# Bias groups in pairs behind the values, first scores before the ninth group, and finishing transposes right behind those of the probabilities

## The chip, the cores and the metric

The kernel runs on one core of a Trainium2 chip. The core has five engines that run at the same time and wait for each other by semaphores: TensorE (PE: matmuls and transposes; PEld is its loading of weights), VectorE (DVE), ScalarE (ACT), GpSimd (POOL) and SyncE (SP), which here issues nearly all transfers between HBM and the on-chip memory SBUF. Matmuls write to PSUM, eight banks per partition; VectorE and ScalarE read them there. The metric is the device time of one execution in microseconds (us), the median of several runs.

## The reference

Attention with a bias that depends on the positions, then two feed-forward layers. B = 2, H = 8, S = 576, D = 64, a hidden size of 32 for the bias.

```python
scores = scale * q @ k^T                                   # per batch and head, 576 x 576
x = log1p(|i - j|) / log1p(max(i, 1))                      # 576 x 576
bias = relu(x * w1 + b1) @ w2                              # 32 hidden, one bias per head
attn = softmax(scores + bias) ; out = attn @ v
x = out as (1152 tokens, 512)
x = (silu(xn @ w_gate) * (xn @ w_val)) @ w_out             # xn: RMS-normed x, 512 -> 1536 -> 512
return (s * relu(x @ w_in)**2 + b) @ w_out2                # 512 -> 2048 -> 512
```

## The kernel before

**Attention.** The work is cut into 36 units: nine tiles of 128 queries, four pairs of heads each (unit u is pair u % 4 of tile u // 4). A loop over steps s = -2 to 36, written out by hand, sets the order on every engine, since each engine runs its instructions in program order. Step s does the scores of unit s + 1 (`scores_mm`, L236, into two PSUM tiles of the ring `psA`), its softmax (`soft` on VectorE, L249, adds the bias and gives the row's extreme; `expo` on ScalarE, L257), the transposes of the probabilities of unit s (`turn_mm`, nine transposes, L266 and L268, in three PSUM tiles; `turn_out`, L274, copies the first and the third to SBUF on ScalarE, the second on VectorE) and the values of unit s - 1 (`values_mm`, L294).

**Finishing a tile of queries.** When the four units of tile p are through, `finish_a` (ScalarE copies `po`, at the start of a step with s % 4 = 1), `finish_t` (four transposes, L307, same step), `finish_b`, `finish_s` and `finish_n` (VectorE: division, norm) and `finish_c` (four transposes back, L339, in a step with s % 4 = 0, from step 8 on) bring the tile into the layout of the feed-forward part.

**PSUM.** The bias groups from 8 on, the transposes of the probabilities and those of the finish all take their tiles from one ring of three buffers, `psB`, in program order: a tile waits until the one three places earlier has been read.

**The bias.** The 576 rows come in 36 groups of 16. `hidden(g)` writes four hidden rows of group g ("quads", L168): on VectorE, but the third on ScalarE for g < 8 and the fourth on GpSimd for g >= 8. `bias_mm(g)` multiplies them with w2 (L181, 8 instructions; the wider g is from the middle, the more columns, 304 to 576), `bias_out(g)` scales them on ScalarE (L197) and stores them: groups 0 to 7 right into the SBUF bias tile (L205), the others to HBM (`rows`, L201), from where a later step's `bias_in` loads them in the shape of the scores (L215). A load waits for the store of its rows. One bias tile serves eight units; its eight groups must be there before the first of them.

**What is in the way of what.** `plan[s]` says which groups' matmuls come in step s: groups 0 to 8 in step -2, then one a step up to group 35 in step 25, at the start of the step, ahead of the scores. SP issues in program order the keys (`load_k`, 288 KB a unit, needed for units 0 to 7), the values (`load_v`, 320 KB), rows (295.5 KB) and bias loads (288 KB a group); an entry that waits holds all behind it.

**Feed-forward.** From about 189 us TensorE does the two feed-forward layers with split weights (L531 to L533); the change doesn't touch them.

Of the kernel before, what the change touches and what calls it, by code (L numbers as in the profile page):

```python
# [8 lines left out]
F32 = mybir.dt.float32  # L9
# [8 lines left out]
P = 128  # L18
# [19 lines left out]
SCALE = 8.0  # L38
AHD = 9
LEAD = 3  # L40
# [9 lines left out]
def tile_kernel(ctx: ExitStack, tc: tile.TileContext, q, k, v, ltab, lg, cst, cst2, rms_g, wg, wv, wo, win, wo2, s_p, b_p, out):  # L50
# [105 lines left out]
    def hidden(g):  # L156
        hms[g] = []
        d = reach(g)
        for tq in range(4):
# [4 lines left out]
            if tq == ACT_QUAD and g in ACT_EARLY:  # L164
                nc.scalar.activation(hq, src, AF.Relu, bias=nthr[:, n:n + 1], scale=w1_sb)
                continue
            eng = nc.gpsimd if tq == POOL_QUAD and g >= 8 else nc.vector
            eng.tensor_scalar(hq, src, w1_sb, thr[:, n:n + 1], op0=ALU.mult, op1=ALU.max)  # L168
# [230 lines left out]
    for g in range(AHD, NG):  # L399
        plan[g - 10 if g >= 16 else g - AHD - 1].append(g)  # L400

    def hide(g):
        if g < NG:
            hidden(g)

    AHEAD = {6: (load_k, 1), 8: (load_v, 0)}
    TAIL = [(22, w_fetch, 0), (22, w_fetch, 1), (27, w_clamp, 0), (28, w_clamp, 1), (31, w_split, 0), (31, w_fetch, 2),
# [3 lines left out]
    for g in range(LEAD):  # L411
        hide(g)
    for s in range(-2, NU + 1):
        r = s % 4
# [8 lines left out]
        landed = list(rows)  # L423
        for g in plan[s]:
            pb = bias_mm(g)
            if g == 0:
                pcb = psB.tile([P, 512], F32, name="b")
                nc.tensor.matmul(pcb[:, 0:1], c2_sb[:, :P], c2_sb[:, P:], start=True, stop=True)
                nc.scalar.activation(cb[:, 0:1], pcb[:, 0:1], AF.Copy, scale=SCALE)
                nc.scalar.activation(cb[:, 1:2], pcb[:, 0:1], AF.Copy, scale=m_sb)  # L430
            bias_out(g, pb)
            if g in AHEAD:
                AHEAD[g][0](AHEAD[g][1])
            if s == -2:
                hide(g + LEAD)
        for g in landed:
            bias_in(g)
        if s >= 6 and r == 2:
            finish_b(s // 4 - 1)
# [20 lines left out]
        if s >= 7 and r == 3:  # L460
            finish_n(s // 4 - 1)
        if plan[s] and s >= -1:
            hide(plan[s][-1] + LEAD)
        if s == 0:
            nc.sync.dma_start(out=g_bc, in_=rms_g.partition_broadcast(P))
            nc.sync.dma_start(out=s_sb, in_=s_p)
            nc.sync.dma_start(out=b_sb, in_=b_p)
        if 0 <= s - 1 < NU:
            values_mm(s - 1)
        if s >= 5 and r == 1:  # L470
# [3 lines left out]
        if s >= 8 and r == 0:  # L474
            finish_c(s // 4 - 2)
        if s == 26:
            gen.close()
            wpools["ab"] = ring(ctx, "wab", 2)
            wpools["sp"] = ring(ctx, "wsp", 4)
# [261 lines left out]
```

## Time and profile before

| | |
|---|---|
| median of 3 runs | 620.36 us (620.31 to 620.48) |
| profiled execution | 620.82 us, of which the span of instructions is 619.0 us |
| mean granted TensorE clock | 0.994 |
| busy, share of the span | TensorE 98%, VectorE 65%, ScalarE 50%, GpSimd 33% |
| HBM | 53.47 MB read, 10.83 MB written |

Times below are us from the span's start. "Idle before" in square brackets is the time the engine stood still ahead of a row, with what ended it. The granted clock is the share of TensorE's full clock of 2.4 GHz; 0.5 is its lower level, 1.2 GHz. Ends of matmuls are modelled, so how long a piece of TensorE's work takes is read from the start of one row to the start of the next.

### The profile page before, as it was taken

What the parts mean: (1) busy time and instruction counts of PE and PEld (TensorE: products, weight loads), DVE (VectorE), ACT (ScalarE), POOL (GpSimd) and SP (SyncE); (2) the same over time, 40 slices, a digit from 0 to 9 for tenths busy, and PEclk for the clock granted to TensorE, in tenths of its full rate; (3) what the DMA queues carried; (4) which work ended last, traced back from release to release, by engine and by line L of the source; (5) the groups of instructions that cost most, each with busy time, mean ns of one, the idle gap of its engine ahead of it and who ended that gap; (6) DMA issues with size and microseconds to landing.
All of it is one profiled execution on the core that took longest, in us unless ns stands there. A gap on an engine that the chain in (4) does not pass through costs nothing.

```text
span 619.0 us, 11231 instructions
## 1 busy us (share of the span) xinstructions
PE 607.4 (98%) x4368; PEld 545.4 (88%) x4368; DVE 403.5 (65%) x748; ACT 309.3 (50%) x644; POOL 204.8 (33%) x180
## 2 busy tenths in 40 slices
PE   8699999999999999999999999999999999999997
PEld 5266666666779999999999999999999999999997
DVE  7587898976787555555545555547777635778841
ACT  7387777777775344434443223225555325555310
POOL 0933355530013333333333233223233423232430
PEclk9799999999999999999999999999999999999999
DMA  5699554558021222222231322222212331221431
GB/s 150 183 304 289 155 153 134 155 179 224 11 69 55 84 88 89 98 68 74 98 102 69 103 76 96 69 69 80 90 69 78 128 103 40 96 69 68 141 100 51
DMA packets 25877, 67.39 MB, mean 109 GB/s; under 512 B 3136, under 2 KB 4704, under 8 KB 25824
## 3 DMA queue, kind: packets, MB, share of 16 engines
q1 hardware_dynamic: 25632, 66.37, 34.3%
q8 instruction: 34, 0.56, 0.4%
q10 hardware_dynamic: 192, 0.31, 0.2%
q14 instruction: 19, 0.16, 0.1%
HBM read 53.47 MB, written 10.83 MB: 104 GB/s over the span
## 4 chain that ended last, share of the span: by engine, by line
PE 75%; DVE 13%; ACT 5%; issue 4%; DMA 1%; POOL 1%; SPq 0%; DVEq 0%; POOLq 0%
PE c L531 9%; PE c L532 9%; PE c L533 9%; PE b L533 7%; PE b L531 7%; PE b L532 7%; PE po L294 6%; PE a L236 6%; PE b L266 5%; DVE f L600 4%; DVE hv L596 4%; PE b L181 3%; ACT f L599 3%; PE po L531 2%; PE po L533 2%
## 5 line engine op out<-in xcount | busy, mean ns | idle before, releaser
L391 POOL TENSOR_TENSOR wlo<-ww,whi 128x512 fp32r<-128x512 f32 x68 | 96.5, 1420 | 101.1 <-ACT whi L390 101.1
L369 POOL TENSOR_SCALAR wa<-wa 128x512 f32<-128x512 f32 x68 | 44.2, 650 | 182.8 <-ACT wa L368 180.3
L168 POOL TENSOR_SCALAR hq<-tab,c_sb,thr 128x448 f32<-128x448 f32 (+17 forms) x28 | 57.7, 2065 | 40.2 <-PE b L181 26.2
L249 DVE CUSTOM_DVE_ANT_0 sn<-a,bias 128x576 f32<-128x576 f32 x72 | 51.7, 753 | 28.5 <-PE a L236 22.8
L375 DVE TENSOR_SCALAR wa<-wa 128x512 int32<-128x512 int32 x68 | 37.6, 553 | 40.1 <-POOL wa L369 40.1
L257 ACT ACTIVATE pr<-sn,nm 128x576 f32<-128x576 f32 x72 | 56.1, 780 | 6.2 <-DVE nm L249 6.1
L368 ACT ACTIVATE wa<-wraw 128x512 f32<-128x512 f32 x68 | 45.3, 666 | 27.4 <-DMA wraw<-in_wo 24.9
L533 PE MATMUL c<-f,wlo 128*128 128x384 f32 (+1 forms) x168 | 55.7, 332 | 0.0
L532 PE MATMUL c<-f,whi 128*128 128x384 f32 (+1 forms) x168 | 55.7, 332 | 0.0
L531 PE MATMUL c<-f,whi 128*128 128x384 f32 (+1 forms) x168 | 55.7, 332 | 0.0
L376 DVE SCALAR_TENSOR_TENSOR ww<-wraw,wa 128x512 int32<-128x512 int32 x68 | 52.7, 775 | 3.5 <-issue 0.4
L600 DVE SCALAR_TENSOR_TENSOR f<-hv,b_sb,f 128x384 fp32r<-128x384 f32 x48 | 39.2, 818 | 21.9 <-ACT f L599 21.9
L378 DVE SCALAR_TENSOR_TENSOR ww<-wraw,ww 128x512 int32<-128x512 int32 x68 | 51.9, 763 | 2.3
L599 ACT ACTIVATE f<-hv,b_sb 128x384 fp32r<-128x384 f32 x48 | 29.6, 617 | 45.1 <-DVE hv L596 45.0
L532 PE MATMUL c<-xs,whi 128*128 128x384 f32 x144 | 48.3, 335 | 0.0
L390 ACT CAST whi<-ww 128x512 fp32r<-128x512 f32 x68 | 41.8, 615 | 12.9 <-DVE ww L378 12.9
L531 PE MATMUL c<-xs,whi 128*128 128x384 f32 x144 | 48.2, 335 | 0.0
L533 PE MATMUL c<-xs,wlo 128*128 128x384 f32 x144 | 48.1, 334 | 0.0
L294 PE MATMUL po<-pt,vs 128*64 128x128 f32 (+1 forms) x800 | 47.3, 267 | 0.0
L236 PE MATMUL a<-ks,q 64*128 64x288 f32 (+1 forms) x320 | 46.4, 432 | 0.0
L533 PE MATMUL b<-f,wlo 128*128 128x384 f32 (+1 forms) x132 | 44.8, 339 | 0.4 <-POOL wlo L391 0.4
L532 PE MATMUL b<-f,whi 128*128 128x384 f32 (+1 forms) x132 | 44.6, 338 | 0.0
(121 smaller groups left out, 1481.7 us busy)
## 6 DMA issues: line engine op xcount, KB each, us to landing
wraw<-in_wo SPq DMA_DIRECT2D x28, 512.0 KB, 3.3
bias<-rows SPq DMA_DIRECT2D x32, 288.0 KB, 4.4
rows<-br SPq DMA_DIRECT2D x28, 295.5 KB, 3.2
wraw<-in_win SPq DMA_DIRECT2D x16, 512.0 KB, 3.3
wraw<-in_wg SPq DMA_DIRECT2D x12, 512.0 KB, 3.3
wraw<-in_wv SPq DMA_DIRECT2D x12, 512.0 KB, 3.3
vs<-in_v SPq DMA_DIRECT2D x8, 320.0 KB, 5.3
ks<-in_k SPq DMA_DIRECT2D x8, 288.0 KB, 5.7
```

Source lines behind the costliest of these rows:

```text
L168: eng.tensor_scalar(hq, src, w1_sb, thr[:, n:n + 1], op0=ALU.mult, op1=ALU.max)
L236: nc.tensor.matmul(ps[e][qc, f, :HF], qt[u // 4][ed, hp, qc], ks[b * NP + hp][ed, f * HF:(f + 1) * HF], start=True, stop=True, tile_positi ...
L249: nc.vector.tensor_tensor_reduce(out=sn, in0=ps[:, :, :HF], in1=bias[chunk(u)][:, h, :].rearrange("p (f c) -> p f c", f=2), scale=-1.0 / S ...
L257: nc.scalar.activation(prs[u][:, e * S:(e + 1) * S], sn.rearrange("p f c -> p (f c)"), AF.Exp, bias=nm, scale=-1.0, accum_out=sums[u // 4] ...
L294: nc.tensor.matmul(dst, w, a, start=c == 0, stop=c == NQC - 1, tile_position=(0, e * D))
L376: yield nc.vector.scalar_tensor_tensor(out=w, in0=raw[:, :, 1], scalar=-0x40000000, in1=a, op0=ALU.bitwise_and, op1=ALU.bitwise_or)
L378: yield nc.vector.scalar_tensor_tensor(out=w, in0=raw[:, :, 0], scalar=29, in1=w, op0=ALU.logical_shift_right, op1=ALU.bitwise_or)
L391: nc.gpsimd.tensor_tensor(out=lo, in0=w.bitcast(F32), in1=hi.bitcast(F32), op=ALU.subtract)
L531: nc.tensor.matmul(ps, hi[:, ws], ah, start=first, stop=False)
L532: nc.tensor.matmul(ps, hi[:, ws], al, start=False, stop=False)
L533: nc.tensor.matmul(ps, lo[:, ws], ah, start=False, stop=last)
L600: nc.vector.scalar_tensor_tensor(out=hl[:, cols(j)], in0=g2, scalar=b_sb, in1=hh[:, cols(j)].bitcast(F32), op0=ALU.add, op1=ALU.subtract)
```

## The change

Four things are moved. (1) Step -2 has groups 0 to 7 only; groups 8 and 9 come in step -1, behind the first scores, and GpSimd writes its quarter of the hidden rows only from group 11 on. (2) From group 10 to 31 two groups come together, in every second step (10 and 11 in step 0, 12 and 13 in step 2, ..., 30 and 31 in step 20); groups 32 to 35 keep their steps. (3) The groups of a step stand at its end, behind the values, not ahead of the scores; hidden rows are written for group s + 12 in step s. (4) `finish_t` and `finish_c` stand ahead of the values, right behind the transposes of the probabilities. The keys of unit 1 are loaded behind group 7 instead of 6, the first values behind group 9 instead of 8.

```diff
-AHD = 9
+AHD = 8
+POOL_FROM = 11
...
-            eng = nc.gpsimd if tq == POOL_QUAD and g >= 8 else nc.vector
+            eng = nc.gpsimd if tq == POOL_QUAD and g >= POOL_FROM else nc.vector
...
-        plan[g - 10 if g >= 16 else g - AHD - 1].append(g)
+        plan[g - 10 if g >= 32 else max(g - g % 2 - 10, -1)].append(g)
...
-    AHEAD = {6: (load_k, 1), 8: (load_v, 0)}
+    AHEAD = {7: (load_k, 1), 9: (load_v, 0)}
...
+    def groups(s):
+        for g in plan[s]:
+            pb = bias_mm(g)
...
+            bias_out(g, pb)
+            if s == -2:
+                hide(g + LEAD)
+            if g in AHEAD:
+                AHEAD[g][0](AHEAD[g][1])
...
-        for g in plan[s]:
-            pb = bias_mm(g)
...
         for g in landed:
             bias_in(g)
+        if s == -2:
+            groups(s)
...
-        if plan[s] and s >= -1:
-            hide(plan[s][-1] + LEAD)
+        if s >= -1:
+            hide(s + 12)
...
-        if 0 <= s - 1 < NU:
-            values_mm(s - 1)
         if s >= 5 and r == 1:
             finish_t(s // 4 - 1)
...
         if s >= 8 and r == 0:
             finish_c(s // 4 - 2)
+        if 0 <= s - 1 < NU:
+            values_mm(s - 1)
+        if s >= -1:
+            groups(s)
```

TensorE at the start, before: the last groups of step -2, the first scores (`ks0`), group 10 at the start of step 0 and so on (line, operation, tile written <- tiles read, shape of the result, count).

```order
L181 MATMUL a<-hq,c_sb 32x512 x4
L181 MATMUL a<-hq,c_sb 32x64 x4
L181 MATMUL b<-hq,c_sb 32x448 x4
L181 MATMUL b<-hq,c_sb 32x432 x4
L236 MATMUL a<-ks_127,q 128x288 x4
L181 MATMUL b<-hq,c_sb 32x416 x4
L236 MATMUL a<-ks_309,q 128x288 x4
L266 MATMUL b<-ident,pr 128x128 x8
L268 MATMUL b<-ident,pr 128x128
L181 MATMUL b<-hq,c_sb 32x400 x4
```

The same place of the changed kernel:

```order
L182 MATMUL a<-hq,c_sb 32x512 x4
L182 MATMUL a<-hq,c_sb 32x64 x4
L237 MATMUL a<-ks_127,q 128x288 x4
L182 MATMUL b<-hq,c_sb 32x448 x4
L182 MATMUL b<-hq,c_sb 32x432 x4
L237 MATMUL a<-ks_337,q 128x288 x4
L267 MATMUL b<-ident,pr 128x128 x8
L269 MATMUL b<-ident,pr 128x128
L182 MATMUL b<-hq,c_sb 32x416 x4
L182 MATMUL b<-hq,c_sb 32x400 x4
```

The first scores have moved ahead of groups 8 (448 columns) and 9 (432), and groups 10 and 11 (416 and 400) stand together behind the transposes of unit 0.

TensorE in a step with `finish_t`, before (`pt` and `vs` are probabilities and values, `oT` the tile that is turned; seven more rows of values are left out):

```order
L236 MATMUL a<-ks_593,q 128x288 x4
L266 MATMUL b<-ident,pr 128x128 x8
L268 MATMUL b<-ident,pr 128x128
L294 MATMUL po<-pt_690,vs_591 64x128
...
L294 MATMUL po<-pt_705,vs_591 64x128 x2
L307 MATMUL b<-ident,oT 128x128 x4
L181 MATMUL b<-hq,c_sb 32x320 x4
L236 MATMUL a<-ks_662,q 128x288 x4
```

A later step of the same kind in the changed kernel:

```order
L182 MATMUL b<-hq,c_sb 32x304 x4
L182 MATMUL b<-hq,c_sb 32x320 x4
L237 MATMUL a<-ks_339,q 128x288 x4
L267 MATMUL b<-ident,pr 128x128 x8
L269 MATMUL b<-ident,pr 128x128
L308 MATMUL b<-ident,oT 128x128 x4
L295 MATMUL po<-pt_948,vs_385 64x128
...
L295 MATMUL po<-pt_963,vs_385 64x128 x2
L237 MATMUL a<-ks_339,q 128x288 x4
```

The four transposes have moved from behind the values to the place right behind the nine of the probabilities; two groups of the bias stand together ahead of this step and none behind it.

SP up to the keys of unit 4 (`ks4`), before, from the store of group 8's rows on (buffer numbers kept; `br` is the scaled group, `g_bc` and two small constants are left out):

```order
L201 DMA rows8_347<-br_344 128x591
L134 DMA vs0_349<-in_v 128x640
L130 DMA ks2_359<-in_k 128x576
L201 DMA rows9_369<-br_366 128x591
L215 DMA bias_371<-rows8_347 16x8x576
L126 DMA q_397<-in_q 128x512
L134 DMA vs1_399<-in_v 128x640
L130 DMA ks3_401<-in_k 128x576
L201 DMA rows10_411<-br_408 128x591
L215 DMA bias_371<-rows9_369 16x8x576
...
L134 DMA vs2_458<-in_v 128x640
L130 DMA ks4_460<-in_k 128x576
```

The same in the changed kernel, from the keys of unit 2 on:

```order
L131 DMA ks2_339<-in_k 128x576
L202 DMA rows8_373<-br_370 128x591
...
L135 DMA vs1_389<-in_v 128x640
L131 DMA ks3_391<-in_k 128x576
L216 DMA bias_393<-rows8_373 16x8x576
L216 DMA bias_393<-rows9_383 16x8x576
...
L202 DMA rows10_448<-br_445 128x591
L202 DMA rows11_458<-br_455 128x591
L135 DMA vs2_460<-in_v 128x640
L131 DMA ks4_462<-in_k 128x576
```

The keys of unit 2 have moved ahead of the first rows, and the rows of group 11 now stand ahead of the keys of unit 4; the other transfers between are the same.

## Rows read from the trace of the kernel before

**Rows 1.** The page: TensorE's busy tenths in 40 slices of the span.

```profile
PE   8699999999999999999999999999999999999997
```

**Rows 2.** Stages: busy us (x instructions) by engine, granted clock, DMA share, GB/s.

```profile
18.00:24.00 6.00, 1.56 (x11) 0.34 (x10) 3.72 (x10) 0.83 (x1) 6.00 (x2) 0.81 0.79 192
...
28.00:42.00 14.00, 13.85 (x128) 8.36 (x125) 12.01 (x30) 10.94 (x28) 7.07 (x5) 0.98 0.98 301
...
64.00:130.00 66.00, 65.96 (x662) 43.99 (x662) 59.39 (x141) 52.46 (x125) 30.25 (x17) 1.00 0.50 147
```

**Rows 3.** Timeline of GpSimd, 15 to 22 us: start, us, instruction, [idle before].

```profile
15.21 8.24 POOL L168 TENSOR_SCALAR hq<-tab,c_sb,thr 128x448 f32<-128x448 f32 x1 [13.89 <-DMA bias<-br]
```

**Rows 4.** Timeline of all engines, 0 to 36 us (x: instructions merged).

```profile
16.71 5.02 DVE L168 TENSOR_SCALAR hq<-tab,c_sb,thr 128x448 f32<-128x448 f32 x12
...
19.10 0.54 SPq L205 DMA_DIRECT2D bias<-br  x1
23.50 0.20 PEld L181 LDWEIGHTS b<-hq,c_sb 128*32 128x32 f32 x8 [5.25 <-POOL hq L168]
...
25.30 1.09 ACT L197 ACTIVATE br<-b,cb,c_sb 128x448 f32<-128x448 f32 x2 [6.34 <-PE b L181]
...
28.97 0.76 DVE L249 CUSTOM_DVE_ANT_0 sn<-a,bias 128x576 f32<-128x576 f32 x1 [7.25 <-PE a L236]
...
30.55 0.76 ACT L257 ACTIVATE pr<-sn,nm 128x576 f32<-128x576 f32 x1
```

**Rows 5.** The bias tile, 0 to 40 us: its transfers from issue to landing.

```profile
DMA to landing us min/median/max: 3.2/4.3/6.3
```

**Rows 6.** Timeline of SP, 0 to 75 us: when transfers are issued.

```profile
26.41 0.34 SPq L201 DMA_DIRECT2D rows<-br  x1
...
36.11 0.33 SPq L130 DMA_DIRECT2D ks<-in_k  x1
```

**Rows 7.** DMA issues of 28 to 62 us: count, KB each, median us to landing.

```profile
ks<-in_k SPq DMA_DIRECT2D x5, 288.0 KB, 5.7
```

**Rows 8.** Timeline of TensorE, 36 to 47 us.

```profile
42.40 1.24 PE L236 MATMUL a<-ks,q 64*128 64x288 f32 x8
...
45.95 0.80 PE L181 MATMUL b<-hq,c_sb 128*32 128x352 f32 x8
46.68 0.51 PE L236 MATMUL a<-ks,q 64*128 64x288 f32 x2
```

**Rows 9.** Timeline of TensorE, 86 to 97 us.

```profile
86.47 0.66 PE L339 MATMUL b<-ident,x 128*128 128x128 f32 x4
87.06 0.85 PE L181 MATMUL b<-hq,c_sb 128*32 128x384 f32 x8
87.84 1.24 PE L236 MATMUL a<-ks,q 64*128 64x288 f32 x8
89.01 1.09 PE L266 MATMUL b<-ident,pr 128*128 128x128 f32 x8
...
90.14 1.31 PE L294 MATMUL po<-pt,vs 128*64 128x128 f32 x20
```

**Rows 10.** Timeline of all engines, 82.8 to 86.5 us: the step before.

```profile
84.84 0.58 ACT L274 COPY pt<-b 128x512 f32<-128x512 f32 x1 [0.67 <-PE b L266]
85.02 0.27 PE L268 MATMUL b<-ident,pr 128*128 128x128 f32 x1
...
85.23 1.31 PE L294 MATMUL po<-pt,vs 128*64 128x128 f32 x20
```

**Rows 11.** Timeline of TensorE, 117 to 124.5 us: a group of 496 columns.

```profile
119.69 1.04 PE L181 MATMUL b<-hq,c_sb 128*32 128x496 f32 x8
120.66 1.24 PE L236 MATMUL a<-ks,q 64*128 64x288 f32 x8
```

**Rows 12.** Timeline of TensorE, 58.5 to 66 us.

```profile
64.13 1.62 PE L236 MATMUL a<-ks,q 64*128 64x288 f32 x8
```

**Rows 13.** Timeline of TensorE, 126 to 192 us.

```profile
140.74 0.29 PE L181 MATMUL b<-hq,c_sb 128*32 128x48 f32 x8 [0.56 <-DVE pt L274]
```

More of the change, by code (lines that the diff above doesn't have):

```diff
@@ L412, in tile_kernel @@
         hide(g)
+    def groups(s):
+        for g in plan[s]:
+            pb = bias_mm(g)
+            if g == 0:
+                pcb = psB.tile([P, 512], F32, name="b")
+                nc.tensor.matmul(pcb[:, 0:1], c2_sb[:, :P], c2_sb[:, P:], start=True, stop=True)
+                nc.scalar.activation(cb[:, 0:1], pcb[:, 0:1], AF.Copy, scale=SCALE)
+                nc.scalar.activation(cb[:, 1:2], pcb[:, 0:1], AF.Copy, scale=m_sb)
+            bias_out(g, pb)
[3 more added lines that the diff above has]
+                AHEAD[g][0](AHEAD[g][1])
     for s in range(-2, NU + 1):
@@ L423, in tile_kernel @@
         landed = list(rows)
-        for g in plan[s]:
-            pb = bias_mm(g)
[L426 to L435, printed above, removed]
         for g in landed:
             bias_in(g)
+        if s == -2:
+            groups(s)
         if s >= 6 and r == 2:
```

## The prediction

> **What bounds the kernel now.** I read the slices of the span first [rows 1]: after the first 40 us TensorE is at 0.9 or more in nearly every slice. The stages say the same [rows 2]: from 64 to 130 us TensorE has work in 65.96 of 66 us while VectorE has 59.39 and ScalarE 52.46. So in the attention steps time is gained or lost where TensorE's own row of work gets longer or shorter, or where something makes it stand still. It stands still at the start: from 18 to 24 us it works 1.56 of 6 us at a granted clock of 0.81, and from 28 to 42 us it is the DMA engines that are full (0.98 of the time, 301 GB/s) [rows 2].
>
> The hole at the start is a chain. GpSimd's first hidden row (group 8) starts at 15.21 and takes 8.24 us [rows 3]: VectorE writes its twelve hidden rows in 5.02 us from 16.71 [rows 4], and GpSimd is done only 1.7 us after that run. TensorE's weight load for group 8 waited 5.25 us for it, until 23.50, and the first softmax piece starts at 28.97, 7.25 us after VectorE fell idle [rows 4].
>
> **Part 1, the start.** Now the four hidden rows of groups 8, 9 and 10 are all VectorE's. That is twelve again (three of four groups before), so they end at about 21.7 as before. The first scores come ahead of groups 8 and 9: they start when group 7 is written out, about 19.1 (the last bias piece is issued at 19.10 [rows 4]), and the first softmax piece then waits for that piece: the median landing of these is 4.3 us [rows 5], so 23.4, at most 25.4 (by 6.3). Against 28.97 this is 5.6 us earlier. It costs something: ScalarE now has the write-outs of groups 8 and 9, 1.09 us each for two instructions [rows 4], behind two exponentials and ahead of the first probability copies, so 5.6 - 2.2 = 3.4 us of head start remain. VectorE's run of twelve then meets a GpSimd row (group 11) at its end at most.
>
> **Part 2, who catches up with the head start.** Every unit of scores needs its keys. The keys of unit 4 are issued at 36.11 [rows 6]; with the median landing of 5.7 us [rows 7] they are there at 41.8, and the scores that read them start at 42.40 [rows 8]: 0.6 us of slack while the DMA engines are full. In the new order of SP the transfers from the first bias rows (group 8) to these keys are the same but two: the keys of unit 2 went earlier, into the gap in which the DMA engines were idle, and the rows of group 11 now stand ahead. Both are some 290 KB, so the full stretch is as long. It starts when the rows of group 8 are stored: before at 26.41 [rows 6], now at 23.4 + 2.3 (from the first softmax piece at 28.97 to the end of the second exponential at 31.31 [rows 4]) + 1.1 = 26.8, some tenths later for the issue. So the keys land at about 42.4 and those scores start at 42.5, against 42.40: the 3.4 us are waited away there. From one set of keys to the next are two bias loads, one load of values and the keys, 1.18 MB, at 301 GB/s 3.9 us: 46.4. A step without bias rows (scores 1.17 and transposes 1.13 by the starts at 87.84, 89.01 and 90.14 [rows 9], values 1.24 from 85.23 [rows 10] to 86.47 [rows 9]) would want them at 42.5 + 3.55 = 46.05. So unit 5 starts at 46.4 with groups 12 and 13 done; before it started at 46.68 with group 14 done too, 0.73 us more work from 45.95 [rows 8]: **+0.45 us**. Bounds: -3.4, if the keys keep pace after all, and +1.5, if the transfers run 1 us later. Later steps alternate between 3.55 us and some 4.8 us, and a wait of some tenths in the short ones is inside those bounds.
>
> **Part 3, the finishing transposes.** Today `finish_t` and `finish_c` stand behind the values and cost TensorE 0.59 us for four transposes (86.47 to 87.06 [rows 9]). Nine in a row take 1.13 us, so one more costs about 0.11 and four more at the end of the nine would cost 0.43. But the PSUM ring `psB` has three buffers. The three tiles of a step's transposes take all three, and the fourth, that of the finishing transposes, is the buffer of the first: it waits until ScalarE has copied that one to `pt0`. Before, the values (1.24 us) stood between and hid this copy. Now nothing does. In the step at 83 us the copy runs from 84.84 to 85.42; the ninth transpose starts at 85.02, and the next work of TensorE, the values, at 85.23 [rows 10]. With the finishing transposes in that place TensorE stands until 85.42, some 0.04 more for the release, and then pays the full 0.59: the values start at about 86.05 instead of 85.23. So a finish costs 0.82 where it cost 0.59: **+0.24 us each**. There are eight of each kind; all but the last `finish_c` (step 36, no transposes of probabilities there) stand in such a place: 15 x 0.24 = **+3.6 us**. That last one now stands between two runs of values, at most one more change of kind, about **+0.15** (0.59 - 0.43). The copy can hardly be earlier: it starts when its four transposes are done (ScalarE was idle before it). It can be later: in the steps of `finish_t` ScalarE first has the copy of `po` behind two write-outs; by the same rows that chain is over when the transposes are, within 0.2 us. Bounds for one finish: -0.16 (no wait) and +0.4.
>
> The Trainium skill (TensorEngine Tiling (Array Packing), Key Properties) says that changing the tiling mode drains TensorE. That agrees with 0.59 us for four transposes by themselves and 0.43 in a row, and by this rule alone part 3 would be a gain of 15 x 0.16 = 2.4 us; by the ring and the copy's rows it is a loss of 3.6.
>
> **Part 4, two groups together.** A group of 384 columns takes 0.78 us (87.06 to 87.84 [rows 9]) and one of 496 columns 0.97 (119.69 to 120.66 [rows 11]): 1.7 ns a column, so 0.65 of the 0.78 grow with the columns and 0.13 are the change of kind before and behind. The second group of a pair saves these 0.13 (0.08 to 0.18, by what a hundredth of a microsecond in each start does). From groups 14 and 15 to groups 30 and 31 these are nine pairs: **-1.2 us** (-0.7 to -1.6).
>
> **Part 5, two waits that go.** The scores of unit 9 took 1.62 instead of 1.24 us at 64.13 [rows 12], held by the softmax of unit 8, which needs the last bias rows of its tile. These are now stored and loaded a step earlier: **-0.38**. At 140.74 the second bank of a group waited 0.56 us for VectorE [rows 13], again behind a late bias load (group 31, issued behind the store of group 32); in pairs it goes a step earlier: **-0.56**. The order of hidden rows (one step closer to their use) and the loads of q move past nothing that waits: TensorE reads those rows two steps later.
>
> **The sum.** 0.45 + 3.6 + 0.15 - 1.2 - 0.38 - 0.56 = +2.1 us. The profiled execution took 620.82 us, so 622.9 by it; against the median of the runs, 620.36, which is 0.46 lower, I forecast **622.4 us**. The feed-forward stages behind are TensorE's from end to end and take the shift as it is.
>
> **Rivals.** (A) The finishing transposes save what their place promises, 0.16 each. Then 15 x -0.16 = -2.4 stands for +3.6 and the sum is -3.9: 616.5 us. For it speaks that transposes in a row are cheap; against it the order of the ring, and the copy that ends 0.19 us after the place is reached. It is what the rule of the Trainium skill in part 3 gives when the copy is in nobody's way. It decides only if the copy ends before 85.2 in a step like that one. (B) The head start is kept: the keys land 3 us earlier than I work out, say because the stores and loads in pairs run faster than 301 GB/s. Then 2.1 - 0.45 - 3.4 = -1.75: 618.6 us; with half of it 620.5. Against it: the DMA engines were full at 0.98 with the same bytes. (C) TensorE's waits for keys bring its clock down again, as 18 to 24 us shows (0.81) [rows 2]: one step at half clock costs 3.5 us more, of which part falls into the next wait: 624 to 626 us.
>
> **Chances.** My forecast 0.58, A 0.12, B 0.18, C 0.12. A measurement of this kernel can tell about 0.2%, 1.24 us. My forecast lies 2.0 above the median; I give 0.09 of its 0.58 to a result within 0.2%. B lies half on the faster side and half within. Faster: 0.12 + 0.09 = 0.21; the same: 0.09 + 0.09 = 0.18; slower: 0.61. The likeliest case alone has 620.9 to 624; the range leaves out A and the worse half of C: 618.4 to 624.8.
>
> **What will show it.** Right: the first softmax piece near 23.5; a wait of TensorE for `ks` near 40 to 42 us and scores of unit 4 near 42.5; in each step with a finish a hole of 0.2 to 0.4 us before it, ended by `pt`, and 0.8 us from the ninth transpose's end to the values; no hole at 140. Wrong: finishing transposes right behind the ninth (A), scores of unit 4 by 40 (B), or a granted clock of half between 40 and 50 us (C).

## The result, and the profile after

| | median us | lowest to highest | runs |
|---|---|---|---|
| kernel before | 620.42 | 620.31 to 622.05 | 4 |
| changed kernel | 627.28 | 626.73 to 628.14 | 4 |

The ratio is 1.0106, 95% interval 1.0085 to 1.0126: slower, as forecast, but by 6.6 us (6.9 by the medians) where 2.1 were worked out. The profiled execution took 627.03 us, 6.2 more than that of before. TensorE's slices and granted clock, from the page (against [rows 1]), differ in the first three slices of 15.6 us: 7 and 8 in the first and third, where 8 and 9 stood; the second is fuller, 7 where 6 stood:

```profile
PE   7789999999999999999999999999999999999997
PEclk9899999999999999999999999999999999999999
```

The first hidden row and the first softmax piece, VectorE's timeline:

```profile
6.67 1.56 DVE L169 TENSOR_SCALAR hq<-near,c_sb,thr 128x576 f32<-128x576 f32 x3 [3.58 <-DMA near<-in_ltab]
...
25.68 0.76 DVE L250 CUSTOM_DVE_ANT_0 sn<-a,bias 128x576 f32<-128x576 f32 x1 [2.18 <-DMA bias<-br]
```

The first hidden row waits for the first table and started 1.74 us later than in the trace of before (4.93), ahead of everything that the change moves (runs 16 to 18 come back to it). Without that the softmax piece stands at 23.9; the forecast was 23.4, against 28.97 before [rows 4]. The head start exists. TensorE's timeline shows where it goes (`nm` is the row's extreme, which the softmax on VectorE writes; scores that take a buffer of `psA` wait for it):

```profile
26.50 2.96 PE L237 MATMUL a<-ks,q 64*128 64x288 f32 x8 [2.91 <-DVE nm L250]
...
44.93 1.24 PE L237 MATMUL a<-ks,q 64*128 64x288 f32 x8 [2.41 <-DMA ks<-in_k]
46.11 1.61 PE L267 MATMUL b<-ident,pr 128*128 128x128 f32 x8
...
47.86 2.31 PE L295 MATMUL po<-pt,vs 128*64 128x128 f32 x20
50.30 1.24 PE L237 MATMUL a<-ks,q 64*128 64x288 f32 x8
```

The scores of unit 4 start at 44.93, not at 42.5, behind a wait of 2.41 us for their keys; they started at 42.40 before [rows 8]. Behind the wait the clock is half: the values took 2.31 us, not 1.31. In this trace that cost nothing, since the keys of unit 5, issued at 44.28, took 5.9 us to land: they were there at 50.2, and the scores start at 50.30. SP's timeline says why the keys are late:

```profile
29.10 1.29 SPq L202 DMA_DIRECT2D rows<-br  x2
...
32.42 1.23 SPq L216 DMA_DIRECT2D bias<-rows  x2
33.70 0.58 SPq L470 DMA_DIRECT2D g_bc<-in_rms_g  x1
...
35.75 0.85 SPq L202 DMA_DIRECT2D rows<-br  x2
37.38 0.33 SPq L135 DMA_DIRECT2D vs<-in_v  x1
38.87 0.33 SPq L131 DMA_DIRECT2D ks<-in_k  x1
42.24 1.36 SPq L216 DMA_DIRECT2D bias<-rows  x2
...
44.28 0.42 SPq L131 DMA_DIRECT2D ks<-in_k  x1
...
50.97 2.25 SPq L216 DMA_DIRECT2D bias<-rows  x2
```

SP issues in order. It stands at the store of group 8's rows until 29.10 with all later loads behind it, and the keys of unit 4 go out at 38.87 (36.11 before [rows 6]). Then the load of group 10's rows waits for their store, which takes 6.5 us to land (35.75 to 42.24 from issue to issue), and the keys of unit 5 stand behind it: 5.4 us from one set of keys to the next (38.87 to 44.28), where 3.9 were worked out. The stages (columns as in [rows 2]) show DMA engines that are not full, where before they were at 0.98 from 28 to 42:

```profile
26.00:30.00 4.00, 3.50 (x11) 2.42 (x12) 3.39 (x10) 3.52 (x8) 0.70 (x1) 0.51 0.02 6
28.00:42.00 14.00, 13.78 (x117) 8.74 (x117) 9.95 (x25) 10.92 (x29) 3.10 (x2) 0.83 0.87 257
42.00:52.00 10.00, 7.46 (x58) 5.51 (x51) 3.60 (x10) 4.33 (x10) 2.89 (x2) 0.83 0.86 274
```

Further on, one step with a finish and one with a full group (TensorE):

```profile
112.39 1.09 PE L267 MATMUL b<-ident,pr 128*128 128x128 f32 x8
113.32 0.27 PE L269 MATMUL b<-ident,pr 128*128 128x128 f32 x1
113.78 0.66 PE L308 MATMUL b<-ident,oT 128*128 128x128 f32 x4 [0.18 <-ACT pt L275]
114.36 1.31 PE L295 MATMUL po<-pt,vs 128*64 128x128 f32 x20
...
138.56 1.11 PE L182 MATMUL b<-hq,c_sb 128*32 128x512 f32 x16
139.61 1.24 PE L237 MATMUL a<-ks,q 64*128 64x288 f32 x8
```

From the ninth transpose to the values it is 1.04 us, against 0.21 without a finish [rows 10]: a finish costs 0.83, and the hole is ended by `pt`; 0.82 was forecast. The hole at 140 [rows 13] is gone.

To tell the parts apart I use three starts of TensorE's timeline in every trace: the scores of unit 4, of unit 9, and the first feed-forward matmul. The kernel before has group 18 done ahead of the scores of unit 9, all kernels below have not (0.65 us); in the last column this is added to the rows of before. Ratios are to the kernel before on the same chip.

| run | first hidden row | unit 4 | unit 9 | unit 9 to feed-forward | ratio, interval |
|---|---|---|---|---|---|
| before (profile above) | 4.93 | 42.40 | 64.13 | 124.86 + 0.65 | 1 |
| before, runs 16, 17, 18 | 5.58, 4.61, 5.34 | 43.13, 43.14, 43.94 | 64.86, 64.86, 65.66 | 124.06 to 124.12 + 0.65 | 1 |
| changed | 6.67 | 44.93 | 67.92 | 127.51 | 1.0106, 1.0085 to 1.0126 |
| 1 changed again | 6.98 | 45.50 | 70.24 | 127.56 | 1.0107, 1.0077 to 1.0138 |
| 2 finish back | 7.21 | 45.92 | 70.38 | 123.64 | 1.0024, 1.0005 to 1.0042 |
| 3 start back | 5.65 | 42.96 | 65.19 | 127.94 | 1.0061, 1.0039 to 1.0083 |
| 4 keys early | 4.86 | 39.15 | 65.25 | 128.27 | 1.0101, 1.0077 to 1.0125 |
| 5 both back | 5.50 | 43.89 | 64.83 | 124.01 | 0.9979, 0.9962 to 0.9996 |
| 6 one values | 4.90 | 41.30 | 63.26 | 127.60 | 1.0026, 1.0012 to 1.0040 |
| 7 busy waits | 6.32 | 45.73 | 70.12 | 127.57 | 1.0125, 1.0097 to 1.0152 |
| 8 ring free | 5.32 | 43.04 | 67.36 | 121.35 | 0.9976, 0.9959 to 0.9993 |
| 9 loads early | 5.30 | 39.46 | 64.17 | 129.41 | 1.0068, 1.0053 to 1.0083 |
| 10 between | 5.70 | 45.29 | 68.02 | 125.66 | 1.0060, 1.0043 to 1.0077 |
| 11 small first | 5.55 | 42.03 | 64.93 | 127.52 | 1.0065, 1.0047 to 1.0083 |
| 12 all new | 4.77 | 38.55 | 62.06 | 127.20 | 1.0006, 0.9987 to 1.0026 |
| 13 early, pairs | 5.31 | 41.56 | 62.91 | 124.29 | 0.9988, 0.9972 to 1.0003 |
| 14 early, singles | 6.19 | 41.63 | 66.84 | 127.43 | 1.0068, 1.0052 to 1.0084 |
| 15 singles, small | 5.90 | 42.30 | 67.62 | 127.24 | 1.0060, 1.0044 to 1.0076 |

### The profile page after: what moved, and what is told of

It is laid out like the page before. It is cut to its first block, busy times and chain, and to the rows that moved or that the text cites. A ratio compares the mean times of both kernels' runs of the same rounds, so it can differ in the third digit from the quotient of the medians.

```text
span 625.2 us, 11230 instructions
## 1 busy us (share of the span) xinstructions
PE 608.2 (97%) x4368; PEld 549.7 (88%) x4368; DVE 403.7 (65%) x751; ACT 307.7 (49%) x644; POOL 192.3 (31%) x177
## 4 chain that ended last, share of the span: by engine, by line
PE 70%; DVE 12%; ACT 9%; issue 4%; DMA 4%; POOL 0%; SPq 0%; DVEq 0%; ACTq 0%
PE c L540 8%; PE c L538 8%; PE c L539 8%; PE b L540 7%; PE b L538 6%; PE b L539 6%; PE po L295 6%; PE a L237 5%; DVE f L607 4%; DVE hv L603 4%; PE b L267 4%; ACT br L198 3%; ACT f L606 3%; PE b L182 2%; PE po L540 2%
## 5 line engine op out<-in xcount | busy, mean ns | idle before, releaser
L392 POOL TENSOR_TENSOR wlo<-ww,whi 128x512 fp32r<-128x512 f32 x68 | 95.2, 1400 | 102.4 <-ACT whi L391 102.4
L169 POOL TENSOR_SCALAR hq<-tab,c_sb,thr 128x400 f32<-128x400 f32 (+17 forms) x25 | 46.4, 1864 | 57.1 <-PE b L182 35.4
L275 ACT COPY pt<-b 128x512 f32<-128x512 f32 x72 | 30.3, 422 | 35.9 <-PE b L267 35.8
L295 PEld LDWEIGHTS po<-pt,vs 128*64 128x64 f32 x800 | 40.2, 139 | 6.2 <-issue 6.2
```

What stands on the lines that cost most here:

```text
L295: nc.tensor.matmul(dst, w, a, start=c == 0, stop=c == NQC - 1, tile_position=(0, e * D))
L392: nc.gpsimd.tensor_tensor(out=lo, in0=w.bitcast(F32), in1=hi.bitcast(F32), op=ALU.subtract)
```

## The experiments

The theory at the outset: finish and start cost about 4 and 3 us, pairs and waits give some 2 back. The rival: the finish costs nothing here and all is lost at the start.

**1. The changed kernel again**, beside the next three. 

> The changed kernel once more. My account of its trace has a loss of about 4.0 us by the scores of unit 9 (late keys, a stretch at half clock, and a first table that landed 1.7 us later than in the trace of before) and about 2.5 us behind them. If the late table was chance, a run without it still loses at least 2.5 us at the start, and the time stays at 626 to 628 us; if the table's lateness is the cause of the early loss, a run without it comes out near 624 us.

It repeats: the same ratio, and three waits for keys in the profiled execution (1.16, 1.76 and 1.87 us). The first table was late again (6.98), so this run can't tell its share from that of the change; runs 8 and 10 can, which have the changed start and an earlier table (5.32 and 5.70): from the first hidden row to the scores of unit 9 they take 62.0 and 62.3 us, this run 63.3 and the trace above 61.25. Here the clock is half behind the wait for unit 5, and no wait follows (TensorE):

```profile
50.99 1.24 PE L237 MATMUL a<-ks,q 64*128 64x288 f32 x8 [1.87 <-DMA ks<-in_k]
52.16 1.83 PE L267 MATMUL b<-ident,pr 128*128 128x128 f32 x8
...
57.45 1.24 PE L237 MATMUL a<-ks,q 64*128 64x288 f32 x8
```

From unit 5 to unit 6 it is 6.46 us, 4.84 in the trace above: the clock cost 1.6 us. Runs 2 and 8 have the same (6.38 and 6.41).

**2. Only the finishing transposes back behind the values.**

```diff
+        if 0 <= s - 1 < NU:
+            values_mm(s - 1)
         if s >= 5 and r == 1:
             finish_t(s // 4 - 1)
...
-        if 0 <= s - 1 < NU:
-            values_mm(s - 1)
```

> Only the finishing transposes go back behind the values; start, pairs and places of the groups stay as changed. My theory (each finish waits for the copy of the first probabilities' tile: 0.84 us at finish_c and 0.84 to 0.99 us at finish_t instead of 0.59): 15 x 0.25 to 0.3 us less and some tenths at step 36, so 4 to 4.7 us less than the changed kernel, near 623 us. Rival A (a finish in the new place saves 0.16 us, the loss is all in the start and in the pairs): 2.4 us more, near 629.5 us.

1.0024 beside 1.0107: some 5 us, 4 to 4.7 expected. The last column is the cleaner measure, since it holds none of the start: 127.5 to 123.6, 3.9 us.

**3. Only the start back** (nine groups ahead, single groups up to 15, the scores behind them; pairs from 16). 

> Everything up to step 5 as before (nine groups first, GpSimd from group 8, one group a step ahead of the scores up to group 15); pairs from group 16 on and finishing transposes as changed. My theory (the start itself loses some 4 us by late keys and half clock): near 622.8 us, with the scores of unit 9 as early as in the kernel before or 0.3 us earlier. Rival (pairs load ScalarE in lumps and that is what costs): the early loss is small and the time stays above 625 us.

1.0061 beside 1.0107: the start costs 2.9 us by the ratios, 3.1 by the medians, where the theory had some 4. Against the kernel before on record then (620.42) its 622.8 us are a ratio of 1.004 and the rival's 625 are 1.007, so the result lies between them. Unit 4 starts where it did before, counted from the first hidden row (37.3 us; 37.5 to 38.6 in the traces of before).

**4. Keys one or two steps earlier on SP.**

```diff
-        if -1 <= s < 5:
-            load_k(s + 3)
+        if -1 <= s < 3:
+            for n in (2, 3, 4) if s < 0 else (s + 5,):
+                load_k(n)
```

> The changed kernel with the keys of units 2 to 4 issued together ahead of the first stored rows, and those of units 5 to 7 two steps earlier; nothing else moved. My theory (TensorE waits for the keys of units 3 to 5 and its clock falls in that wait): the waits at 37 and 42 us and the stretch at half clock go, 2.5 to 4 us less, near 624 us. Rival (the head start is lost to ScalarE's order or to the bias loads, not to the keys): the wait moves to values or bias rows and the time changes by less than 1 us.

A miss for the theory of late keys alone: the time is as with run 1. The wait went to the next thing in SP's queue, the values (TensorE's timeline):

```profile
42.38 1.31 PE L295 MATMUL po<-pt,vs 128*64 128x128 f32 x20 [0.86 <-DMA vs<-in_v]
...
47.99 1.31 PE L295 MATMUL po<-pt,vs 128*64 128x128 f32 x20 [1.99 <-DMA vs<-in_v]
```

**5. Start and finish both back**: what is left are the pairs from group 16 on (runs 2 and 3 together). 

> Here the start and the place of the finishing transposes are those of the kernel before; what is left of the change is the pairs of groups from group 16 on and the two waits that go with them. If the three parts add up (start about +3, finish about +5, pairs and waits -1.5), this kernel is 1.5 us faster than before, a ratio near 0.9976; after the scores of unit 9 it takes about 1.5 to 1.9 us less than before to the feed-forward stage, and the group 31 wait of TensorE (0.56 us at 140) is gone. Rival: the pairs gain nothing by themselves (the row of transposes and groups only changes its order), ratio 0.9995 to 1.0005, and the gain seen without the finish was another run's chance.

0.9979, 1.3 us less than before: the parts add within their errors, and this part of the change is a gain by itself. Behind unit 9 it takes 1.5 us less than the first trace of before, as expected, but only 0.7 less than the later ones (runs 16 to 18).

**6. One load of values for all units.**

```diff
         if 0 <= s < 7:
-            load_v(s + 1)
+            vs[s + 1] = vs[0]
```

> The changed kernel with the values of unit 0 used in all eight places: seven loads of values (320 KB each, 2.3 MB) are not made, so the output is not that of the reference. If the transfers are what catches up with the head start, the keys of unit 4 (behind three loads of values) land 2 us earlier and those of later units 3 us and more, the scores of unit 4 start near 42.5 instead of 44.9 and no wait for keys over 0.5 us follows; the kernel is 4 to 6 us faster than the changed one, a ratio to the kernel before of 1.001 to 1.004. Rival: the loss lies in the start itself (the first table late, the two write-outs of groups 8 and 9 ahead of the first copies): the scores of unit 9 start at most 1 us earlier than in the changed kernel and the ratio stays at 1.009 to 1.011.

1.0026 beside 1.0107: 5 us, as expected of a start bound by transfers. But the waits for keys, which were to go, are still there, 1.81 (below, TensorE) and 0.71 us, and while TensorE stands in the first of them the DMA engines are at 0.42 (the stage's row):

```profile
41.30 1.24 PE L237 MATMUL a<-ks,q 64*128 64x288 f32 x8 [1.81 <-DMA ks<-in_k]
```
```profile
38.00:42.00 4.00, 2.19 (x24) 1.10 (x24) 1.02 (x3) 2.73 (x6) 2.90 (x2) 1.00 0.42 141
```

So it is not bytes alone: something holds the transfers back while the engines that move them are idle. This led to runs 9 to 15.

**7. TensorE kept busy in the waits ahead of units 0 and 4.**

```diff
+BUSY = {0: 10, 4: 9}
...
+        for _ in range(BUSY.get(u, 0)):
+            nc.tensor.matmul(ps[0][:, 0, :P], ident, ident, start=True, stop=True)
```

> The changed kernel with 10 matmuls of the identity ahead of the scores of unit 0 and 9 ahead of those of unit 4, about 2 us each at full clock, in the places where TensorE waits 2.9 and 2.4 us. They write the bank that the scores overwrite. If the fallen clock is a cost of its own, the granted clock stays full from 26 to 33 us and from 46 to 50 us, and the kernel is 1 to 2 us faster than the changed one (3.4 us at half clock are 1.7 us of work): ratio 1.007 to 1.009. Rival: the transfers alone set the pace, and work that runs at full clock waits the longer for the next keys: the clock is full, but the next wait for keys (unit 5 or 6) grows by as much and the ratio stays within 0.001 of 1.0107. A third outcome: the clock falls all the same, then these matmuls don't settle it.

The granted clock is 1.00 from 28 to 52 us, and the kernel is no faster (1.0125). As the rival has it, the next wait grows, to 3.14 us (TensorE):

```profile
43.52 2.27 PE L235 MATMUL a<-ident 128*128 128x128 f32 x18
45.73 1.24 PE L240 MATMUL a<-ks,q 64*128 64x288 f32 x8
...
52.49 1.24 PE L240 MATMUL a<-ks,q 64*128 64x288 f32 x8 [3.14 <-DMA ks<-in_k]
```

Work that is done sooner waits the longer here. But that the clock is free is not shown: the keys of unit 5 took 7.3 us from issue to landing, where it was 5.9 in the changed kernel and 5.6 in run 1, so part of the longer wait is their later landing. Whether these matmuls have to do with that stays open.

**8. A buffer of the ring left free in the steps with a finish.**

```diff
-            for e in (1, 2):
-                turn_out(s, e, turn_mm(s, e))
+            turn_out(s, 1, turn_mm(s, 1))
+            if (s >= 5 and r == 1) or (s >= 8 and r == 0):
+                pts[s, 2] = last2
+            else:
+                turn_out(s, 2, turn_mm(s, 2))
+                last2 = pts[s, 2]
```

> The changed kernel, but in the fifteen steps with finishing transposes the ninth transpose of the probabilities and its copy are left out (the values read the tile of the step before, so the output is not that of the reference). So the finishing transposes take the third buffer of the ring and not the first one again. If their cost in the new place is the wait for the copy pt0, the hole ahead of them goes, the values start about 0.45 to 0.5 us behind the eighth transpose, and each of the fifteen steps is 0.11 (the transpose) plus 0.3 to 0.4 us shorter: 6 to 7.5 us less than the changed kernel, ratio 0.9985 to 1.001. Rival: four finishing transposes cost some 0.6 us wherever they stand and the hole is only where an unavoidable drain shows: then only the left-out transposes count, 15 x 0.11 = 1.7 us less, ratio near 1.008.

The hole is gone (TensorE, the step that stands above at 112.39):

```profile
109.34 1.09 PE L267 MATMUL b<-ident,pr 128*128 128x128 f32 x8
110.27 0.60 PE L308 MATMUL b<-ident,oT 128*128 128x128 f32 x4
110.80 1.31 PE L295 MATMUL po<-pt,vs 128*64 128x128 f32 x20
```

Eight transposes and the four of the finish take 1.46 us to the values, where nine alone take 1.13 [rows 9]: 0.11 for each further one. The changed kernel takes 1.97 for thirteen, which would be 1.57: the hole costs 0.40. In all it is 127.5 to 121.35 in the last column, 6.2 us, of which 1.5 are fourteen transposes left out; 4.7 remain for fourteen holes, 0.33 each. One of the fourteen finishes has another wait in its place (0.50 us for VectorE at 186.84). By the ratios the gain is 8.1 us, above the 6 to 7.5 expected, but with an error of some 2 us.

**9. Six loads ahead of the first store.**

```diff
-        if 0 <= s < 7:
-            load_v(s + 1)
-        if -1 <= s < 5:
-            load_k(s + 3)
+        if s == -1:
+            for n, fn in ((2, load_k), (0, load_v), (3, load_k), (1, load_v), (4, load_k), (2, load_v)):
+                fn(n)
+        if 0 <= s < 5:
+            load_v(s + 3)
+        if 0 <= s < 3:
+            load_k(s + 5)
```

> The changed kernel with the loads of keys 2, 3, 4 and values 0, 1, 2 ahead of the store of group 8's bias rows on SP, and all later keys and values two steps earlier. In the changed kernel the DMA engines moved 6 GB/s from 26 to 30 us, since SP stood at that store (issued 29.10) and all loads are queued behind it. If this standing queue is what cost the head start, the loads fill that gap: no wait of TensorE for keys or values over 0.5 us between 30 and 60 us, scores of unit 4 within 15 us of those of unit 1 (18.4 in the changed kernel), no half clock after 35 us, and 3 to 4.5 us less than the changed kernel: ratio 1.0035 to 1.006. Rival: the bytes of the stage bound it wherever the loads stand (as when the keys alone went earlier): the wait only moves to the bias rows and the softmax behind them, ratio 1.009 to 1.011.

Half of the theory and half of its rival: 2.4 us less than run 1, 3 to 4.5 expected. No wait for keys or values is left between 30 and 60 us, unit 4 starts 14.2 us behind unit 1, and unit 6 at 47.85 (50.93 before): 3 us of head start. Then TensorE stands 3.48 us ahead of the scores of unit 9, behind the softmax of unit 8, which needs the rows of groups 14 and 15 (TensorE's row, then two of SP's):

```profile
64.17 2.35 PE L237 MATMUL a<-ks,q 64*128 64x288 f32 x8 [3.48 <-DVE nm L250]
```
```profile
52.20 0.86 SPq L202 DMA_DIRECT2D rows<-br  x2
57.94 1.19 SPq L216 DMA_DIRECT2D bias<-rows  x2
```

Behind that wait TensorE's granted clock is 0.50 (66 to 68 us), and unit 10 comes 7.47 us behind unit 9, 5.57 in the changed kernel: the 1.9 us by which the last column is longer (129.41).

**10. Finishing transposes ahead of the ninth, not behind it.**

```diff
+            turn_out(s, 1, turn_mm(s, 1))
+            if s >= 5 and r == 1:
+                finish_t(s // 4 - 1)
+            if s >= 8 and r == 0:
+                finish_cm(s // 4 - 2)
+            turn_out(s, 2, turn_mm(s, 2))
+            if s >= 8 and r == 0:
+                finish_co(s // 4 - 2)
```

(`finish_cm` and `finish_co` are the transposes of `finish_c` and the two operations that read them.) 

> The changed kernel with the finishing transposes ahead of the ninth transpose of the probabilities in place of behind it, so that they take the third buffer of the PSUM ring and the single transpose takes the first one again; nothing is left out. If the wait for the copy pt0 is the cost, eight transposes (0.93 us) now lie over that copy (0.6 us), the hole goes, and each of the fifteen steps is some 0.40 us shorter: 5 to 6 us less than the changed kernel, ratio 1.001 to 1.0035. From the ninth step's scores on it should take some 121.5 to 122.5 us to the feed-forward stage (127.5 in the changed kernel, 123.6 with the finish behind the values). Rivals: the hole moves to the single transpose, or the finishing transposes now wait for ScalarE's copy of po or for the normalized x, which had one transpose more time before: ratio 1.006 or more.

Less than the 5 to 6 us expected: 2.9 by the ratios (1.0060), 1.9 in the last column (125.66). The hole is gone from its place, but the work that takes the next tiles of the ring is longer: a pair of 432 columns behind a finish takes 1.94 us, 1.68 in the changed kernel, and the next step's transposes 1.29, not 1.09 (TensorE):

```profile
109.43 1.94 PE L182 MATMUL b<-hq,c_sb 128*32 128x432 f32 x16
...
113.40 0.60 PE L308 MATMUL b<-ident,oT 128*128 128x128 f32 x4
113.86 0.33 PE L269 MATMUL b<-ident,pr 128*128 128x128 f32 x1
114.12 1.31 PE L295 MATMUL po<-pt,vs 128*64 128x128 f32 x20
...
116.53 1.29 PE L267 MATMUL b<-ident,pr 128*128 128x128 f32 x8
```

By the ring's order these wait for buffers that the finish and the ninth transpose hold; the trace doesn't name what ended them. Of the orders tried here with four tiles through three buffers, only that with 1.2 us of values between has no such wait.

**11. The three small loads at the program's start.** 

> The changed kernel with the three small loads (g_bc, s_sb, b_sb) moved from step 0 to the program's start on SP. In the changed kernel they are issued at 33.70 and take 7 to 8 us to land, and the load of group 10's bias rows, next but four on SP, is issued only at 42.24; the keys of unit 5 stand behind it. If such landings hold SP, that load is issued near 39 to 40 and the keys of unit 5 some 2 us earlier; the wait for unit 4 (2.41) and the one for unit 5 shrink: 1 to 2.5 us less, ratio 1.0065 to 1.009. Rival: SP waits for the store of those rows or for full DMA engines: the same issue times within 0.7 us, ratio 1.010 to 1.011.

The time is as expected (1.0065), the reason only in part. The load of group 10's rows still goes out 6.6 us behind their store (33.14 to 39.72): it is the store that SP waits for, as the rival has it. What the edit gave is that this store, and the keys of unit 4 (35.03, not 38.87), are issued earlier: the three issues take SP 2 us by themselves.

**12. Edits 9, 10 and 11 together.** 

> All three edits together (loads ahead of the first store, finishing transposes ahead of the ninth, small loads at the start) in the changed kernel: the version that the runs so far point to. If the parts add up, the head start of about 3.4 us is kept, the finish costs 0.44 in place of 0.59 (-2.2), pairs and waits give their -1.9: 6 to 7.5 us less than before, ratio 0.988 to 0.9905. Rival: the loads still bound the start, then -2.2 and -1.9 stand against some +3: ratio 0.997 to 1.000.

1.0006: near the rival's 0.997 to 1.000, for another reason. Unit 4 starts at 38.55, and the head start is lost at the softmax of unit 8 again: 2.59 us of wait ahead of unit 9 and half clock behind it.

**13 to 15. What holds unit 8.** 13 is edit 9 with edit 2; 14 also writes groups 10 to 15 out one a step; 15 adds edit 11.

```diff
-        plan[g - 10 if g >= 32 else max(g - g % 2 - 10, -1)].append(g)
+        plan[g - 10 if g >= 32 else max(g - 10 - (g % 2 if g >= 16 else 0), -1)].append(g)
```

> The changed kernel with the loads ahead of the first store (as e9) and the finishing transposes behind the values (as e2). The parts found apart should add: e9 took 2.5 us from the changed kernel and e2 some 5: ratio 0.9980 to 1.0005. Scores of unit 7 near 52, and then the hole of 2 to 4 us before the scores of unit 9, ended by VectorE's softmax of unit 8, with the loads of groups 14 and 15 issued some 5 us behind their stores. Rival: the hole in e9 was chance and is not there: ratio 0.9925 to 0.995.

> As e13, but groups 10 to 15 are written out one a step, group 10 in step 0 to group 15 in step 5, as in the kernel before; pairs only from group 16 on. If the pairs of the first steps make unit 8's bias rows late (SP stands for a pair's stores to land before it can issue their loads and what follows), the hole before the scores of unit 9 shrinks below 1 us, the head start of some 3 us reaches those scores (61 to 62 us), and the kernel is 2 to 3.5 us faster than e13: ratio 0.9930 to 0.9955. Rival: group 15, now a step later, makes unit 8 as late or later, or the bytes bound it: ratio within 0.0015 of e13.

> As e14, with the three small loads at the program's start in place of step 0 (as e11). Where e14 still waits for bias rows or keys, SP comes free some 2 us earlier behind step 0: 0.5 to 1.5 us less than e14, ratio 0.991 to 0.9945. Rival: nothing waits there any more, or the 256 KB at the start delay the first bias rows: the same as e14 within 0.0010, or up to 1 us slower.

13 came out as expected (0.9988), but of the hole of 2 to 4 us only 0.48 is left: the loads go out 1.35 us earlier than in run 9, and TensorE comes to unit 8 1.7 us later. 14 is a miss in sign: single groups are some 5 us slower than pairs. Its rival names the cause, though not the size: group 15, a step later, makes unit 8 later. Run 13 (SP, then TensorE) and run 14 (likewise):

```profile
51.05 0.90 SPq L202 DMA_DIRECT2D rows<-br  x2
56.59 1.35 SPq L216 DMA_DIRECT2D bias<-rows  x2
```
```profile
62.91 1.91 PE L237 MATMUL a<-ks,q 64*128 64x288 f32 x8 [0.48 <-DVE nm L250]
```
```profile
58.88 1.04 SPq L202 DMA_DIRECT2D rows<-br  x1
62.47 0.54 SPq L216 DMA_DIRECT2D bias<-rows  x1
```
```profile
66.84 2.96 PE L237 MATMUL a<-ks,q 64*128 64x288 f32 x8 [3.44 <-DVE nm L250]
69.73 1.97 PE L267 MATMUL b<-ident,pr 128*128 128x128 f32 x8
```

From the store of group 15's rows to the scores of unit 9 it is 8 us in run 14 and 11.9 in run 13, in both behind a softmax that waits for them. The wait is half of what run 14 loses: from the first hidden row to the scores of unit 9 it takes 3.1 us more than run 13. The other half lies behind it, 3.1 us in the last column: the clock is half (granted 0.50 from 68 to 74 us), and unit 10 starts only at 75.95, 9.1 us behind unit 9, where run 13 takes 6.15 and run 2 5.3. So pairs in the first steps are no fault but a help: they bring these rows a step earlier. In the kernel before the same softmax holds the scores of unit 9 (1.62 us [rows 12]). That a head start gets past it once the rows of group 15 come earlier still is to be expected, but no run shows it. 15 changed nothing further (1.0060).

**16 to 18. The kernel before, three more traces.** 

> The kernel before, profiled again. If the time at which the first table lands is a draw of each execution, the first hidden row starts anywhere from 4.8 to 7.2 us in these three traces, later than 5.3 in at least one, and the whole trace moves with it. If it comes with the changed kernel, all three lie within 0.3 us of 4.93.

> As e16: a second trace of the kernel before, for the spread of the first hidden row's start (4.8 to 7.2 us if it is a draw, 4.6 to 5.2 if it belongs to the kernel).

> As e16: a third trace of the kernel before, for the same spread.

First hidden rows at 5.58, 4.61 and 5.34: it is a draw in the kernel before too (and 4.77 to 7.21 in the changed kernel and its variants). That draws over 6 us come as often with the kernel before was not shown. The three traces also show two other draws. The hole at 140 [rows 13] is in none of them; run 16:

```profile
139.80 1.15 PE L181 MATMUL b<-hq,c_sb 128*32 128x512 f32 x16
```

And in two of them, and in run 5, the scores of unit 4 do wait for their keys (0.68, 0.64 and 0.61 us): the slack of 0.6 us in [rows 8] was at its end in other executions.

## Why the forecast was right in sign and wrong in size

**Part 1 held.** The first softmax piece came at 23.9 when the late table is taken off (23.7 in run 4, 24.1 in run 6), and the second exponential and the write-out put the store of group 8's rows 3.4 us behind it, as worked out (25.68 to 29.10).

**Part 2 failed, behind unit 4.** From the first hidden row to the scores of unit 4 it said 37.6 us (42.5 less 4.93); the changed kernel took 38.3 and 38.5, before 37.5 to 38.6 in four traces. That half was close: the head start is gone there, as it said. The step that failed is the next, the term of +0.45 us: it took the pace of the keys as bytes over bandwidth, 1.18 MB from one set of keys to the next at 301 GB/s, so unit 5 at +3.9 us, and put what SP stands at a store at nothing. (A KB of the rows is 1024 bytes, so it is 1.21 MB and 4.0 us; that is not what failed.) Unit 5 came at +5.4 and +5.5 (runs: changed, 1; 4.3 before), with the DMA engines at 0.86 and not full: SP stood for a store to land, with the keys behind it. In run 1 unit 6 came another 6.5 us later (4.3 before), at half clock in that step. To the scores of unit 9, from the first hidden row, before took 59.2 to 60.3 us, 59.1 in the mean less the 0.65 of group 18; the changed kernel took 61.25 and 63.26: 3.2 more. Parts 2 and 5, the one finish and the two pairs ahead of unit 9 had put 0.45 - 0.38 + 0.24 - 0.26 = 0.05 there, and the bound of part 2 was +1.5. Run 4 shows that moving the keys alone does not help, run 6 that bytes are part of it, run 9 that the queue is: with six loads ahead of the store, the waits up to 60 us went. The Trainium skill (DMA: Bandwidth & Descriptors, Anatomy of one DMA — SWDGE (gpsimd) path) says that DMA engines do not wait for semaphores, but the sequencer that issues does; that stands in its section on transfers from GpSimd. The trace agrees for those from SP: 6 GB/s from 26 to 30 us, while SP stood at a store with loads behind it.

**Part 3 held.** 0.24 for each finish and 3.75 in all were forecast, 3.5 of it behind the scores of unit 9; run 2 measures 3.9 there. The cause is the ring, as run 8 shows by leaving a buffer free, and run 10 by moving the wait. The Trainium skill (Perfetto Trace Analysis, Optimization Strategy) says that a gap that repeats can mean a lack of SBUF or PSUM for the next tile. The trace agrees: this one repeats in 14 steps from 70 us on, each time until ScalarE has read `b` into `pt`, and is gone in run 8. Rival A's price was right too (13 transposes in a row would take 1.57, so a finish 0.44), only its condition was not met.

**Part 4 held**: nine pairs were to save 1.2 us, the seven of them behind unit 9 0.9; run 2 against the mean of before's later traces saves 124.7 - 123.6 = 1.1 there, run 5, with the same order from there on, 0.7.

**Part 5 was half a draw.** The wait of 0.56 us at 140 was in one of four traces of before, and the longer scores at 64 in three of four. The forecast took one execution's waits for the kernel's.

**Rival B** was the head start kept; it named faster transfers. Runs 9 and 13 show what it takes: loads issued ahead of the store, and rows in time for unit 8. **Rival C**'s mark came (a granted clock of 0.57 from 46 to 50), and its 624 to 626 us are nearer to the measured time than the forecast. What the clock costs depends on what follows: nothing in the changed kernel's trace, where the next keys landed only as the step ended, 1.6 us in run 1, where no wait followed. Run 7 takes the half clock away and gains nothing, but its keys also came later; how much of the 3.2 us is the clock's stays open.

**The sum as measured:** +3.2 for the start, +3.9 for the finish behind unit 9, -1.1 for pairs: +6.0, and 6.6 by the ratios. The rest, 0.6, may be the first table's draw or the error of the ratios (1.3 to 1.9 us either way); it stays open.

The best version that ran and leaves nothing out is run 5, pairs alone: 0.9979, under both kernels. Run 13 has the head start, reaches unit 9 1.2 us ahead of the first trace of before (0.6 of it group 18, which is still to do), and ends at 0.9988, not told apart from run 5.

## What to carry to other kernels

When work is moved ahead, follow the in-order queue that feeds it, instruction by instruction, with what each waits for: a store that waits for a result, or a load that waits for a store, holds every load behind it, and no bandwidth figure shows that. Count the buffers of a ring against the tiles of the new order before counting cheaper instructions; here another place for the fourth tile moved the wait and did not remove it (run 10). A wait of TensorE can cost more than its length when its clock falls in it and no other wait follows (run 14). A wait that a forecast takes away should first be seen in more than one execution.

## What the hardware showed that was not expected

From the issue of the store of a group's rows to that of the load which needs them it took 6.5 us while the DMA engines were busy (35.75 to 42.24, share 0.87) and 3.6 where they were less so (58.88 to 62.47 in run 14, share 0.47). TensorE at a granted clock of 0.57 (46 to 50 us) cost nothing in the changed kernel's trace, since the next keys landed only at 50.2; at 0.50 behind the wait ahead of unit 9 (68 to 74 us in run 14) most of 3.0 us against run 13 is its cost (9.1 and 6.15 us from unit 9 to unit 10). And the landing of the first table, at the program's start, moved whole traces by up to 2.6 us (first hidden row 4.61 to 7.21).
